# A fused attention and gated-MLP block: paired crossbar transposes of the gate/up results, TensorE kept busy before the first tile, and a replanned engine order

## The chip, the cores and the metric

The kernel runs on one core of a Trainium2 chip. Five engines work side by side, each through its own instruction queue in the order in which the queue was filled: TensorE (PE) for matmuls, ScalarE (ACT) for activations, VectorE (DVE) for elementwise work, GpSimd (POOL) for small jobs, and SyncE (SP), which here only issues DMA transfers. An instruction waits on semaphores until what it needs is done, and everything behind it in its queue waits too. The metric is the time of one execution on the device in microseconds; lower is better.

## The reference

A block of one sequence of 2048 tokens with 1024 features, in bfloat16. First comes attention with 32 query heads of width 32 that share one key and one value head, then a gated MLP with 3584 hidden features. Both have a layer norm ahead and a residual around them:

```python
x = A_x                                   # [1, 2048, 1024]
n = layernorm(x)
q, k, v = n @ wq, n @ wk, n @ wv          # q: 32 heads of 32; k and v: one head of 32
p = softmax(q k^T * 32**-0.5)
h = x + concat(p v) @ wo
m = layernorm(h)
out = h + (sigmoid(m @ w_gate) * (m @ w_up)) @ w_down
```

## The kernel before, in words

The 2048 tokens are 16 tiles of 128. The program is first written as a plan: each operation is put in a list of its engine with what it depends on. A planner, the class `Plan`, gives each one a start and an end by durations that are written in the source, and so decides the order in every queue. Only the order and the dependencies reach the chip; planned idle time does not. `TUNE` holds the planner's settings, `LATE` and `SLOW` its corrections for the landing of DMA transfers. `late` is added to every planned landing.

**Head.** Each x tile is loaded, its mean and variance are taken (`stats`), it is centered (`center`, L386) and scaled (L393 or L398). The first four tiles are transposed on PE against an identity (`mk_xT`, L457), the rest by a DMA through the crossbar (L401). From the transposed tiles PE makes K and V (`mk_KV`) and the queries (`mk_Qc`, `mk_Q`).

**Middle.** Attention goes over 512 visits: 32 half tiles of queries (128 tokens by 16 of the 32 heads, 2048 columns in all) by 16 key tiles. A visit (`emit_S`) is four matmuls of 32 rows by 512 columns that run side by side in the four row groups of the array, here called an S round. They fill four PSUM banks with scores, and two ACT instructions of 1024 columns take the exponential of them (L690) into a slot of `Pr`. There are six such banks, so an S round waits for the first exp of the visit before it. DVE adds the exps up (`make_add`, L665). PE multiplies them with V in four column groups (`mk_PV`), sums the partial sums with a small selection matrix (`mk_SUM`), and the reciprocal goes through DRAM (`r_scratch`) to be spread over the partitions (`rb`). `OT` is the product (L748), and `mk_OP` the output projection. Then come the second layer norm and a transposing DMA into `hnT` (`load_hT`).

Between the S rounds PE works on the MLP of earlier tiles. One pass is the MLP of one token tile. It has seven groups of 512 hidden features, each with a gate half and an up half (`mk_GU`), so 14 halves. A half needs one slab of weights of 1 MB, loaded in four pieces (L929) into a ring of four slabs. Odd passes go through the groups in reverse order, and the slabs of a pass's last two groups are kept for the next. A gate half ends with a tanh on ACT (L972), an up half with a product on DVE (L988) into a staging buffer `act_s`. From there a transposing DMA (L991) takes it to `hact`. The first pass and the last two work with the transposed product instead and need no such DMA (`held_w`). The down projection (`mk_D`) takes four pieces of 28 matmuls of 256 columns from `hact` and `wd_sb`; DVE adds each to the residual (L1025), and the rows are stored.

All these groups take one of two PSUM banks (`F_ps`) and are picked by the loop at the end of the kernel. It asks at each step whether an S round can go, or which group's inputs are known to be there by the plan. When a pass starts, `start_ffn` puts due marks for the previous tile's down pieces: a piece comes up when no more gate/up halves are left than its mark plus `d_off`.

**Tail.** After the last S round what remains is the last half tile's sums and output projection and the MLP of the last tiles.

The product that ends an up half, and the DMA behind it:

```python
so = act_s[:, k % NST, :]
e = pl.op("dve", lambda: DVE.scalar_tensor_tensor(
    out=so, in0=tnh[:, :], scalar=1.0, in1=F_ps[:, b, :],
    op0=ALU.add, op1=ALU.mult), [last, box["a"], act_dma.get(k - NST)], prio=0, **t_dve(512))
done = act_dma[k] = dma(lambda: SP.dma_start_transpose(ho, so), ...)
```

Of the kernel before, what the change touches and what calls it, by code (L numbers as in the profile page):

```python
# [12 lines left out]
P = 128  # L13
# [2 lines left out]
SEM = 75.0  # L16


TUNE = dict(late=100, ws0=1, ws1=2, parts0=3, parts1=4, lord=2, h_ord=0, ho=0, ho2=3, pvl1=0, pvl2=0, col_ok=0,
            pace0=310, swait=100, parts=2, raw=1, rl=0, nd=4, pc=16, rate=315, pace=310, xd=4, qf=1, dall=1,  # L20
            wo_late=1, nkn=1, few=1, rmin=600, hmin=1, h0=0, h1=350, hf=1.0, run=700, sum_few=1, pv_few=4,
            d_off=2, d_a=1, d_b=1, eb=0, eq=100)


class Op:
# [16 lines left out]
class Plan:  # L42
# [3 lines left out]
    LATE = {"sl": 465.0, "hT": -90.0, "xt": 100.0, "wd": -100.0, "xr": -300.0, "rb": -250.0, "ql": -500.0, "qs": -200.0,  # L46
            "o": -500.0, "wo": 700.0, "x": -435.0}

    SLOW = {"rb": 1.9, "ha": 2.5, "ql": 1.6, "wq": 1.1}

    def __init__(self):
        self.lists = {e: [] for e in ("pe",) + self.ENG}
        self.free = {e: 0.0 for e in ("pe",) + self.ENG}
        self.heap = {e: [] for e in self.ENG}
        self.dma_free = 0.0
        self.pace_free = 0.0
        self.pe_mode = "dense"
        self.hold = (0.0, 0.0)
        self.t_last = 1e12
        self.seq = 0  # L60

    def op(self, eng, fn, deps=(), order=(), occ=60.0, lat=None, prio=5, key=None, nbytes=0, pace=False, tag=None):
        self.seq += 1
# [38 lines left out]
    def step(self, limit):  # L102
        best = None
        for e in self.ENG:
            h = self.heap[e]
            if h:
                s = min(self.start_of(o) for o in h)
                if best is None or s < best[0]:
                    best = (s, e)
        if best is None or (limit is not None and best[0] > limit):  # L110
            return False
        s, e = best
        h = self.heap[e]
        o = min((o for o in h if self.start_of(o) <= s + 1e-9), key=lambda o: (o.prio, o.seq))
        h.remove(o)
        if o.pace and self.pace_free > s:
            s2 = self.pace_free
            prev = [a for a in self.lists["act"][-6:] if a.end <= s2]
            if prev:
                o.deps.append(prev[-1])  # L120
            s = s2
        self.free[e] = s + o.occ
        o.start = s
        if o.nbytes:
            if o.pace:
                self.pace_free = s + o.nbytes / TUNE["pace0" if self.fast(s) else "pace"]
            k = o.key.rstrip("0123456789_")
            go = max(s + 1720.0, self.dma_free)
            self.dma_free = go + o.nbytes * self.SLOW.get(k, 1.0) / TUNE["rate"]
            o.end = self.dma_free + 700.0 + self.LATE.get(k, 0.0) + TUNE["late"]  # L130
        else:
            o.end = s + o.lat
        o.pos = len(self.lists[e])
        self.lists[e].append(o)
        for u in o.users:
            u.ready = max(u.ready, o.end)
            u.missing -= 1
            if u.missing == 0:
                self.heap[u.eng].append(u)
        o.users = []  # L140
        return True
# [21 lines left out]
def bass_sequential_preLN__grouped_kv_mqa__glu_gated_glu__prompt_kernel(  # L163
# [20 lines left out]
    NH = NT * 2  # L184
    NB = 3
    NHB = 3
    NST = 3
    NSLAB = 4
    SW = 512
    NGR = NFT // 4  # L190
# [4 lines left out]
    with ExitStack() as es:  # L195
# [3 lines left out]
        def SB(name, shape, dt=BF16):  # L199
            return EC(nc.sbuf_tensor(name, [P] + shape, dt))  # L200

        ident = SB("ident", [P])
# [11 lines left out]
        rb = SB("rb", [512], F32)  # L214
# [4 lines left out]
        hnT = SB("hnT", [DT, 2, P])  # L219
        hact = SB("hact", [NFT * 256])  # L220
        tnh = SB("tnh", [512], F32)
        act_s = SB("act_s", [NST, 512])
        st = SB("st", [8, 2, 6], F32)
        mv = SB("mv", [2, NT, 2], F32)
        mvb = SB("mvb", [2, NT, 2])
# [8 lines left out]
        F_ps = EC(nc.psum_tensor("F_ps", [P, 2, 512], F32))  # L234
# [28 lines left out]
        PE, ACT, DVE, POOL, SP = nc.tensor, nc.scalar, nc.vector, nc.gpsimd, nc.sync  # L263

        def dma(fn, key, nbytes, deps=(), prio=5, pace=False, order=(), occ=450.0):
            return pl.op("sp", fn, deps, occ=occ, key=key, nbytes=nbytes, prio=prio, pace=pace, order=order)
# [9 lines left out]
        def both(out_ap, in_ap):  # L276
# [7 lines left out]
        c_id = pl.op("pool", lambda: POOL.affine_select(  # L284
            out=ident[:, :], in_=ident[:, :], compare_op=ALU.not_equal, fill=1.0, base=0,
            pattern=[[-1, P]], channel_multiplier=1), [c2], occ=300)
# [89 lines left out]
        sv1 = {}  # L376
        xnorm = {}
        xcent = {}

        def center(t):  # L380
            if t >= TUNE["pc"]:
                xcent[t] = pl.op("pool", lambda t=t: POOL.tensor_scalar(
                    out=x_sb(t), in0=x_sb(t), scalar1=mvr[:, 0, t, 0:1], scalar2=None, op0=ALU.subtract),
                    [sv1[t][0]], prio=2, occ=1150, lat=1300)
            else:
                xcent[t] = pl.op("dve", lambda t=t: DVE.tensor_scalar(  # L386
                    out=x_sb(t), in0=x_sb(t), scalar1=mvr[:, 0, t, 0:1], scalar2=None, op0=ALU.subtract),
                    [sv1[t][0]], prio=2, occ=330, lat=500)

        def make_norm1(t, deps):  # L390
            dst, src, sc = xn[:, t % 2, :], x_sb(t), rstd[:, 0, t:t + 1]
# [4 lines left out]
        def x_by_dma(t):  # L396

            xnorm[t] = pl.op("dve", lambda: DVE.tensor_scalar(  # L398
                out=x_sb(t), in0=x_sb(t), scalar1=rstd[:, 0, t:t + 1], scalar2=None, op0=ALU.mult),
                [xcent[t], sv1[t][1]], prio=1, occ=330, lat=500)  # L400
            xT_ev[t] = dma(lambda: SP.dma_start_transpose(xnT[:, t // 4, :, (t % 4) * P:(t % 4 + 1) * P], x_sb(t)),  # L401
                           f"xt{t}", P * D * 2, [xnorm[t]], prio=0, occ=1250.0)
            ring_free(t)
            queue_after_xT(t)
            if t == NT - 1:
                load_wo()
# [6 lines left out]
        for tiles in ([0], [1], [2, 3], [4, 5], [6, 7], [8, 9], [10, 11], [12, 13], [14, 15]):  # L413
            after = ((), ())
            if tiles[0] in (1, 2):

                p = tiles[0] - 1
# [19 lines left out]
        def mm(o, l, r, start, stop, **kw):  # L437
            return lambda: PE.matmul(o, lhsT=l, rhs=r, start=start, stop=stop, **kw)  # L438

        def pe_op(fn, n, mode, deps, last_of_round=True):  # L440
            if mode != pl.pe_mode:
                pl.free["pe"] += SWITCH
                pl.pe_mode = mode
            if mode == "dense":
                occ = max(25.0, n / 2.4 + 2.4)
            else:
                occ = max(25.0, n / 2.4 + 2.4) - 10.5 if last_of_round else 3.5
            return pl.op("pe", fn, deps, occ=occ, lat=max(25.0, n / 2.4 + 2.0) + 170.0 + SEM)


        xT_ev = {}
# [448 lines left out]
        def group_of(p, i):  # L900
            return i if p % 2 == 0 else NGR - 1 - i
# [35 lines left out]
        hact_ev = {}  # L937
        box = {}

        act_dma = {}  # L940
        n_act = [0]

        def gu_deps(t):
            return [d_last[t - 2]] if t >= 2 else q_store[-NQS:] if t else extra_rel
# [4 lines left out]
        def mk_GU(t, i):  # L949


            gr = group_of(t, i)
            held_w = t < TUNE["ws0"] or t >= NT - TUNE["ws1"]
            ho = hact[:, :].rearrange("p (a f b) -> p a f b", a=2, b=P)[:, t % 2, 4 * gr:4 * gr + 4, :]
# [22 lines left out]
            def after_u(b, last):  # L977
                if held_w:
                    e = pl.op("dve", lambda: DVE.scalar_tensor_tensor(
                        out=ho, in0=tnh[:, :].rearrange("p (f b) -> p f b", b=P), scalar=1.0,  # L980
                        in1=F_ps[:, b, :].rearrange("p (f b) -> p f b", b=P),
                        op0=ALU.add, op1=ALU.mult), [last, box["a"]] + gu_deps(t), prio=0, **t_dve(512))
                    done = e
                else:
                    k = n_act[0]
                    n_act[0] += 1
                    so = act_s[:, k % NST, :]
                    e = pl.op("dve", lambda: DVE.scalar_tensor_tensor(  # L988
                        out=so, in0=tnh[:, :], scalar=1.0, in1=F_ps[:, b, :],
                        op0=ALU.add, op1=ALU.mult), [last, box["a"], act_dma.get(k - NST)], prio=0, **t_dve(512))  # L990
                    done = act_dma[k] = dma(lambda: SP.dma_start_transpose(ho, so), f"ha{t % 2}_{gr}", P * 1024, [e] + gu_deps(t),  # L991
                                            prio=0, occ=700.0)
                box["e"] = e
                for f in range(4):
                    hact_ev[(t, 4 * gr + f)] = done
                free(1, last)
                if i == NGR - 1:
                    gu_last[t] = last
                    load_hT(t + 2)
                    for dq in range(ND):  # L1000
                        queues["D"].append(mk_D(t, t, dq))
                return [e]
# [63 lines left out]
        while True:  # L1066
            t = pl.free["pe"]
# [204 lines left out]
```

## Time and profile before

| | us |
|---|---|
| time, median of 3 (1107.64 to 1110.86) | 1107.84 |
| span of the profiled execution | 1107.7 |
| PE busy | 1079.6 |
| ACT busy | 1007.6 |
| DVE busy | 842.7 |
| exp on ACT (L690), 1008 of the 1024 | 947.2 |
| gate/up matmuls of 512 columns, 1456 | 362.2 |
| down-projection matmuls, 1792 | 228.6 |
| S matmuls, 2048 | 202.0 |

Instructions of one engine overlap in the pipeline, so the sum of single durations is above the time that a group takes. The 16 DMA engines are busy for 78.2% of the span with the queue that SyncE fills, and 232.92 MB move. The TensorE clock that the throttle granted is full in all slices.

### The profile page before, as it was taken

How to read it: one execution, taken by the hardware profiler on the slowest of the kernel's cores; microseconds unless marked ns; L12 is line 12 of the kernel's file. 1: busy time of each engine (PE TensorE's matmuls, PEld its weight loads, DVE VectorE, ACT ScalarE, POOL GpSimd, SP SyncE). 2: the span in 40 equal slices, each digit the busy share in tenths (PEclk: the TensorE clock that was granted, in tenths of full speed). 3: DMA queues.
4: the chain of work that ended last, by engine and by line, in shares of the span. 5: the costliest groups of instructions: out<-in, count | busy, mean ns of one | idle time of the engine just before them, and what ended most of it. 6: DMA issues, size and time to landing. Idle time of an engine off the chain costs nothing.

```text
span 1107.7 us, 25728 instructions
## 1 busy us (share of the span) xinstructions
PE 1079.6 (97%) x10616; PEld 531.7 (48%) x10616; DVE 842.7 (76%) x1051; ACT 1007.6 (91%) x1155; POOL 65.5 (6%) x93
## 2 busy tenths in 40 slices
PE   6899999999999999999999999999999999999999
PEld 5533365444444444444444443444444444445898
DVE  7979888787878778787878778787877778787311
ACT  4999999999999999999999999999999999998010
POOL 3300000010100001010100101010100101010000
PEclk9999999999999999999999999999999999999999
DMA  8693499787978697696879697697879778686992
GB/s 243 119 314 121 119 322 263 221 218 187 237 186 220 171 263 194 194 226 185 233 178 245 162 241 201 180 221 207 222 186 245 187 201 219 176 227 186 295 324 74
DMA packets 294053, 232.92 MB, mean 210 GB/s; under 512 B 97072, under 2 KB 280368, under 8 KB 293936
## 3 DMA queue, kind: packets, MB, share of 16 engines
q1 hardware_dynamic: 293936, 231.28, 78.2%
q8 instruction: 84, 1.38, 0.5%
q14 instruction: 33, 0.27, 0.1%
HBM read 203.82 MB, written 8.12 MB: 191 GB/s over the span
## 4 chain that ended last, share of the span: by engine, by line
PE 54%; ACT 34%; DMA 5%; DVE 4%; issue 2%; SPq 1%; POOL 0%; DVEq 0%
PE F_ps L438 45%; ACT Pr L690 32%; PE S_ps L438 8%; DMA ring<-in_B_w_up_dram 3%; ACT tnh L972 2%; DVE acc L665 1%; DVE st L342 1%; DMA r_scratch<-r_sb 1%; DVE st L344 0%; DMA zone<-ring 0%; DVE ring L398 0%; DVE ring L386 0%; DMA ring<-in_A_x_dram 0%; DMA rb<-r_scratch 0%; DVE r_sb L731 0%
## 5 line engine op out<-in xcount | busy, mean ns | idle before, releaser
L690 ACT ACTIVATE Pr<-S_ps 128x1024 bf16<-128x1024 f32 x1008 | 947.2, 1076 | 8.0 <-PE S_ps L438 7.5
L665 DVE TENSOR_TENSOR acc<-acc,Pr 128x2048 bf16<-128x2048 bf16 x429 | 524.0, 1221 | 78.4 <-ACT Pr L690 63.3
L438 PE MATMUL F_ps<-ring,hnT 128*128 128x512 bf16 x1456 | 362.2, 381 | 3.9 <-DMA ring<-in_B_w_up_dram 3.0
L438 PE MATMUL F_ps<-zone,hact 128*128 128x256 bf16 x1792 | 228.6, 273 | 0.0
L438 PE MATMUL S_ps<-QTb,kT 32*128 32x512 bf16 x2048 | 202.0, 384 | 5.2 <-ACT Pr L690 3.3
L438 PEld LDWEIGHTS F_ps<-ring,hnT 128*128 128x128 bf16 x1456 | 123.3, 97 | 171.6 <-issue 53.1
L438 PEld LDWEIGHTS F_ps<-zone,hact 128*128 128x128 bf16 x1792 | 163.1, 98 | 63.4 <-issue 32.7
L438 PEld LDWEIGHTS S_ps<-QTb,kT 32*128 32x128 bf16 x2048 | 51.5, 91 | 179.8 <-ACT Pr L690 132.9
L438 PE MATMUL F_ps<-Pr,Vt 128*32 128x512 bf16 x2016 | 135.2, 382 | 0.5 <-DVE Vt L278 0.5
L972 ACT ACTIVATE tnh<-F_ps 128x512 f32<-128x512 f32 x112 | 72.4, 646 | 61.9 <-PE F_ps L438 61.9
L438 PE MATMUL F_ps<-zone 128*128 128x512 bf16 (+3 forms) x584 | 78.5, 281 | 3.9 <-DVE mvb L351 1.4
L988 DVE SCALAR_TENSOR_TENSOR act_s<-tnh,F_ps 128x512 bf16<-128x512 f32 x91 | 62.3, 685 | 22.5 <-PE F_ps L438 20.9
L438 PEld LDWEIGHTS F_ps<-Pr,Vt 128*32 128x32 bf16 x2016 | 43.8, 95 | 60.8 <-issue 28.5
L438 PE MATMUL F_ps<-wo_sb,OT 128*128 128x512 bf16 x256 | 63.6, 381 | 2.0 <-DVE OT L748 1.5
L365 POOL TENSOR_SCALAR zb<-mvb 128x1 bf16<-128x1 bf16 (+1 forms) x23 | 6.0, 260 | 970.0 <-DVE mvb L351 970.0
L438 PE MATMUL F_ps<-hnT,ring 128*128 128x128 bf16 x912 | 61.0, 219 | 0.9 <-DMA ring<-in_B_w_gate_dram 0.7
L438 PEld LDWEIGHTS F_ps<-hnT,ring 128*128 128x128 bf16 x912 | 52.4, 98 | 9.3 <-issue 7.6
L438 PEld LDWEIGHTS F_ps<-zone 128*128 128x128 bf16 x584 | 40.5, 100 | 34.1 <-issue 11.2
L790 DVE TENSOR_TENSOR oun<-F_ps,oun 128x512 f32<-128x512 f32 x34 | 23.5, 691 | 39.8 <-PE F_ps L438 39.8
L1025 DVE SCALAR_TENSOR_TENSOR h_sb<-F_ps,h_sb 128x256 bf16<-128x256 f32 x64 | 26.8, 419 | 30.2 <-PE F_ps L438 30.2
L731 DVE RECIPROCAL r_sb<-F_ps 128x64 f32<-128x64 f32 x31 | 17.3, 558 | 30.8 <-PE F_ps L438 30.7
L438 PEld LDWEIGHTS F_ps<-wo_sb,OT 128*128 128x128 bf16 x256 | 20.9, 97 | 34.4 <-issue 13.1
(73 smaller groups left out, 408.3 us busy)
## 6 DMA issues: line engine op xcount, KB each, us to landing
ring<-in_B_w_gate_dram SPq DMA_DIRECT2D x308, 256.0 KB, 4.7
ring<-in_B_w_up_dram SPq DMA_DIRECT2D x304, 256.0 KB, 4.3
rb<-r_scratch SPq DMA_DIRECT2D x124, 64.0 KB, 2.3
zone<-in_B_w_down_dram SPq DMA_DIRECT2D x14, 512.0 KB, 5.5
Pr<-in_B_w_up_dram SPq DMA_DIRECT2D x24, 256.0 KB, 5.3
Pr<-in_B_w_gate_dram SPq DMA_DIRECT2D x20, 256.0 KB, 5.5
ring<-in_A_x_dram SPq DMA_DIRECT2D x16, 256.0 KB, 5.7
h_sb<-in_A_x_dram SPq DMA_DIRECT2D x16, 256.0 KB, 4.2
```

Source lines behind the costliest of these rows:

```text
L342: a = pl.op("dve", lambda s=s, src=src: DVE.bn_stats(st[:, s, 0, :], src[:, 0:512]), dp, prio=prio, occ=600, lat=756, order=[st_user.get(s ...
L365: f = pl.op("pool", lambda: POOL.tensor_scalar(out=zb[:, ph, tk], in0=mvb[:, ph, tk, 1], scalar1=LN_EPS_BF16, scalar2=None, op0=ALU.add), ...
L438: return lambda: PE.matmul(o, lhsT=l, rhs=r, start=start, stop=stop, **kw)
L665: add_op[(hf, kt)] = pl.op("dve", lambda: DVE.tensor_tensor(out=a, in0=in0, in1=slot, op=ALU.add), dp, prio=6, **t_dve(2048, 1.92))
L690: exps[u] = pl.op("act", lambda i=i, pb=pb: ACT.activation(out=slot[:, i * 1024:(i + 1) * 1024].rearrange("p (a b) -> p a b", a=2), in_=S_ ...
L731: rc = pl.op("dve", lambda: DVE.reciprocal(r_sb[:, :], F_ps[:, b, 0:64]), [last, rd_ld.get(hf - 1)], prio=0, occ=64 * 8 / 0.96 + 20, lat=6 ...
L790: oun_ev[(hf, part)] = pl.op("dve", lambda: DVE.tensor_tensor(out=o, in0=F_ps[:, b, :], in1=o, op=ALU.add), [last, oun_ev[(hf, part - 1)]] ...
L972: box["a"] = pl.op("act", lambda: ACT.activation(out=tnh[:, :], in_=F_ps[:, b, :], func=ACTF.Tanh, scale=0.5), [last, box.get("e")], prio= ...
L988: e = pl.op("dve", lambda: DVE.scalar_tensor_tensor(out=so, in0=tnh[:, :], scalar=1.0, in1=F_ps[:, b, :], op0=ALU.add, op1=ALU.mult), [las ...
L1025: e = pl.op("dve", lambda: DVE.scalar_tensor_tensor(out=h_sb[:, t % NHB, sl], in0=F_ps[:, b, 0:DW], scalar=0.5, in1=h_sb[:, t % NHB, sl], ...
```

## The change

Three things are done together.

1. The results of two neighbouring gate/up groups go into one staging buffer of 1024 columns, and one transposing DMA takes both to `hact`. The seventh group goes alone. There are two such buffers (`NST = 2`) in place of three of half the width. It is meant to halve the number of transposes.
2. Right after the identity matrix is made, PE runs 70 matmuls of 128 columns on it into an unused bank. They are to keep it busy until the first x tile comes.
3. The planner's settings and durations are new. The planned landings are later by 300 ns (`late`), a planned gate/up half waits for two weight pieces (`nkn=2`), planned pacing of weight loads is slower (`pace`), the order of DVE's work on the first two tiles is another (`ho`, `ho2`), and the marks for the down pieces are another (`d_off`, `d_a`, `d_b`). With them the order in all queues is planned anew.

```diff
-TUNE = dict(late=100, ws0=1, ws1=2, parts0=3, parts1=4, lord=2, h_ord=0, ho=0, ho2=3, pvl1=0, pvl2=0, col_ok=0,
-            pace0=310, swait=100, parts=2, raw=1, rl=0, nd=4, pc=16, rate=315, pace=310, xd=4, qf=1, dall=1,
-            wo_late=1, nkn=1, few=1, rmin=600, hmin=1, h0=0, h1=350, hf=1.0, run=700, sum_few=1, pv_few=4,
-            d_off=2, d_a=1, d_b=1, eb=0, eq=100)
+TUNE = dict(warm=70, late=400, ws0=1, ws1=2, parts0=3, parts1=4, lord=2, h_ord=0, ho=3, ho2=0, pvl1=0, pvl2=1,
+            col_ok=1, pace0=310, swait=400, parts=2, raw=1, rl=0, nd=4, pc=16, rate=315, pace=280, xd=4, qf=1,
+            dall=0, wo_late=1, nkn=2, few=1, rmin=900, hmin=1, h0=0, h1=600, hf=1.35, run=700, sum_few=2,
+            pv_few=4, d_off=1, d_a=-1, d_b=-1, eb=150, eq=1000)
...
-    SLOW = {"rb": 1.9, "ha": 2.5, "ql": 1.6, "wq": 1.1}
+    SLOW = {"rb": 1.9, "ql": 1.6, "wq": 1.1}
...
+        self.free["sp"] = self.free["pool"] = 700.0
...
-            self.dma_free = go + o.nbytes * self.SLOW.get(k, 1.0) / TUNE["rate"]
+            w = self.SLOW.get(k, 1.0) if k != "ha" else 2.5 if o.nbytes < 200000 else 1.3
+            self.dma_free = go + o.nbytes * w / TUNE["rate"]
...
-    NST = 3
+    NST = 2
...
-        act_s = SB("act_s", [NST, 512])
+        act_s = SB("act_s", [NST, 1024])
...
-                    [sv1[t][0]], prio=2, occ=330, lat=500)
+                    [sv1[t][0]], prio=2, occ=392, lat=560)
...
-                [xcent[t], sv1[t][1]], prio=1, occ=330, lat=500)
+                [xcent[t], sv1[t][1]], prio=1, occ=392, lat=560)
...
+        for i in range(TUNE["warm"]):
+            pe_op(mm(F_ps[:, 1, 0:P], ident[:, :], ident[:, :], True, True), P, "dense", [c_id] if i == 0 else [])
...
+                    j = i // 2
+                    members = [group_of(t, x) for x in (2 * j, 2 * j + 1) if x < NGR]
+                    g0, n = min(members), len(members)
                     k = n_act[0]
-                    n_act[0] += 1
-                    so = act_s[:, k % NST, :]
+                    if gr == members[-1]:
+                        n_act[0] += 1
+                    so = act_s[:, k % NST, (gr - g0) * 512:(gr - g0 + 1) * 512]
...
-                    done = act_dma[k] = dma(lambda: SP.dma_start_transpose(ho, so), f"ha{t % 2}_{gr}", P * 1024, [e] + gu_deps(t),
-                                            prio=0, occ=700.0)
+                    if gr == members[0] and n == 2:
+                        box["p"] = e
+                        done = None
+                    else:
+                        src = act_s[:, k % NST, 0:512 * n]
+                        hv = hact[:, :].rearrange("p (a f b) -> p a f b", a=2, b=P)[:, t % 2, 4 * g0:4 * (g0 + n), :]
+                        done = act_dma[k] = dma(lambda: SP.dma_start_transpose(hv, src), f"ha{t % 2}_{g0}_{n}", P * 1024 * n,
+                                                [e] + ([box["p"]] if n == 2 else []) + gu_deps(t), prio=0, occ=1245.0)
```

More of the change, by code (lines that the diff above doesn't have):

```diff
@@ L990, in after_u @@
                         op0=ALU.add, op1=ALU.mult), [last, box["a"], act_dma.get(k - NST)], prio=0, **t_dve(512))
-                    done = act_dma[k] = dma(lambda: SP.dma_start_transpose(ho, so), f"ha{t % 2}_{gr}", P * 1024, [e] + gu_deps(t),
-                                            prio=0, occ=700.0)
+                    if gr == members[0] and n == 2:
[6 more added lines that the diff above has]
+                                                [e] + ([box["p"]] if n == 2 else []) + gu_deps(t), prio=0, occ=1245.0)
+                        for g in members:
+                            for f in range(4):
+                                hact_ev[(t, 4 * g + f)] = done
+                if held_w:
+                    for f in range(4):
+                        hact_ev[(t, 4 * gr + f)] = done
                 box["e"] = e
-                for f in range(4):
-                    hact_ev[(t, 4 * gr + f)] = done
                 free(1, last)
```

## The prediction

> **What bounds the kernel now.** I read the page's busy shares and slices first, then the waits, then the head and the tail in the timeline, and last the spacing of single instructions.
>
> ```profile
> PE 1079.6 (97%) x10616; PEld 531.7 (48%) x10616; DVE 842.7 (76%) x1051; ACT 1007.6 (91%) x1155; POOL 65.5 (6%) x93
> ...
> PE   6899999999999999999999999999999999999999
> ...
> ACT  4999999999999999999999999999999999998010
> ```
>
> ACT is full from the second slice to the 37th and then nearly empty. So there are three parts. The head ends at the first S matmul (15.08 us), the middle at the last one (1019.95), and the tail is everything after. They last 15.1, 1004.9 and 87.7 us. The change has to be priced in each.
>
> ```profile
> PEld S_ps L438 <- ACT Pr L690: 132.9, 355, 1.4
> ...
> PEld F_ps L438 <- DMA ring<-in_B_w_up_dram: 12.4, 19, 1.3
> ```
>
> These are waits. Most S rounds wait for an exp to free their PSUM banks, so PE usually leads ACT. But in the trace's starts the lead is short. An S round that waited stands 1.28 us after the start of the exp that freed its banks. The next visit's first exp comes 0.54 us after that S at the most, and never under 0.446 us. So PE leads by only 0.1 us: a visit with 0.12 us too much matmul shows at once as idle ACT. The second line is a different wait: gate/up matmuls that stand for weights still in flight.
>
> ```profile
> 684.92 1.90 PE L438 MATMUL F_ps<-ring,hnT 128*128 128x512 bf16 x8
> 687.30 0.39 PE L438 MATMUL F_ps<-ring,hnT 128*128 128x512 bf16 x1 [0.48 <-DMA ring<-in_B_w_up_dram]
> 687.62 0.39 PE L438 MATMUL S_ps<-QTb,kT 32*128 32x512 bf16 x4
> 687.95 0.39 PE L438 MATMUL F_ps<-ring,hnT 128*128 128x512 bf16 x1
> 688.62 0.60 PE L438 MATMUL F_ps<-ring,hnT 128*128 128x512 bf16 x2 [0.28 <-DMA ring<-in_B_w_up_dram]
> ```
>
> In the timeline of PE the S round stands behind the late gate/up matmul in the fixed order, so a late slab delays the exps too.
>
> **A ledger of the middle.** The middle has 512 visits of one S round. From starts in the trace: a dense matmul takes 216 ns (512 columns), 109 (256) or 56 (128); a round of four packed PV or S matmuls 216; a change between packed and dense 100; about 15 more per visit. ACT takes 911 per exp and 480 per tanh. I count each visit's matmuls from the instruction order, start S no sooner than 1.28 us after the previous visit's first exp, and the exp no sooner than 0.446 us after S. For the kernel before this gives PE 983, ACT 983 and 994.5 us for both together; 64 visits in the steady part give 124.8, and the trace has 125.1 to 127.2. It puts idle ACT where the trace has it (visits 266, 268, 273: 107, 121, 73 ns by ledger, 115, 114, 66 measured). The 10.4 us that it leaves out are 3.4 in the first 64 visits and 7.0 later. The later part is almost the 6.9 us by which 20 gate/up matmuls start later than their spacing, nearly all waiting for weights.
>
> [...] 128-column matmuls start 107 ns apart until 14.2 us and 56 apart after 15.4. [...] weight pieces of 256 KB land 2.8 to 6.0 us (5th to 95th percentile) after issue.
>
> **Head: +0.3.** 70 constant matmuls start when the identity is ready (1.8 us). Priced at 107 ns until the clock rises, and 56 after, [...] I take 8.8, with about the 6.3 us that the clock took in this trace. The first x tile's transposes started at 8.02:
>
> ```profile
> 8.02 1.03 PE L457 MATMUL F_ps<-ident,zone 128*128 128x128 bf16 x8 [8.02 <-DVE zone L393]
> ...
> 9.88 4.64 PE L438 MATMUL F_ps<-zone 128*128 128x128 bf16 x48 [0.83 <-issue]
> ```
>
> Warm, this stretch gives back some 2.5 us (about 48 spacings of 51 ns saved). But the new order (ho=3) puts a BN_STATS of tile 1 (0.61) before tile 0's aggregation, and tile 1's centering before the copy out of PSUM. It also puts tile 1's transposes and K/V (16 further matmuls of 128 columns, then 8 of 32) and two DVE copies ahead of the first S. Following the DVE list by its measured durations, the second Q copy ends near 15.2. First S at 15.1 to 15.8, I take 15.4; the bounds for the sum are -0.5 and +1.2.
>
> **Middle: -5.7.** Three edits act here.
> - The new order: 1136 mode changes where there were 1160, and 29 fewer down-projection matmuls before the last S. PE's ledger falls to 977. Four small evacuations leave ACT (18 to 14, two of them 512 wide), so ACT's falls to 982. Both together: 993.8 against 994.5. The steady 64 visits stay at 124.8: the cuts fall differently, but their imbalances are as large. So the order itself gives 0.7.
> - Pairing: 91 transposes become 39 of two groups and 13 of one. SyncE spent 1.2 us issuing each, so 39 x 1.2 = 47 us of its queue go. The transpose also waits in that queue for its DVE result (62.9 us over 55 waits), with weight loads queued behind it. A pair needs the width of the hnT transpose, which lands in 5.4 us, against 4.1 for one group. The first half also waits for the second group, some 9 us (two of 14 slabs in a 62.8 us pass). The down projection waits for that, but its first piece now starts with 11 of 14 gate/up halves left, where it was 13: three slabs of 4.5 us after the pass, so I price it at nothing. The two wider staging buffers wait for a transpose issued one pair earlier, again some 9 us: nothing.
> - Later planned landings (100 to 400 ns, a first wait for two weight pieces, down-projection pieces spread evenly between slabs): PE gets other work where it stood. Taking 0.3 us off each of the 20 late starts leaves 1.9 of the 6.9 us. Slower planned pacing (310 to 280) is in the same plan. Bounds: all gone, or all kept.
>
> Keeping the 3.4 of the first visits and 0.1 unexplained: 993.8 + 3.4 + 1.9 + 0.1 = 999.2, against 1004.9.
>
> **Tail: +2.4.** PE is dense here, with one gap of size, for the softmax sums' trip through DRAM.
>
> ```profile
> 1034.47 1.11 PE L438 MATMUL F_ps<-hnT,Pr 128*128 128x128 bf16 x17
> 1037.06 1.89 PE L438 MATMUL F_ps<-wo_sb,OT 128*128 128x512 bf16 x8 [1.48 <-DVE OT L748]
> ```
>
> After the last S stand 318 down-projection matmuls where there were 289; the rest is equal: 29 x 109 ns = +3.2. Between the sums and the output projection now lie 29 of 256 columns and 128 of 128, with the sums' own matmuls 10.8 us, against a need of 11.7, so the 1.64 us gap falls to about 0.9. The last hidden state landed 9.5 us after the projection; 128 x 56 + 28 x 109 ns = 10.2 us cover it. +3.2 - 0.8 = +2.4, bounds 1.5 and 3.5.
>
> Sum: 1107.84 + 0.3 - 5.7 + 2.4 = **1104.8 us**.
>
> **Rivals.**
> - Weights as late as before. For it: the loads wait for PE to free a slab (168 us in SyncE's waits), and no more slabs are given; the wait could move with the plan. Against it: the stalls are 0.2 to 0.95 us, the size of the new margin. Then only the ledger's 0.7 counts: 1107.84 + 0.3 - 0.7 + 2.4 = 1109.8.
> - The start smooths out as well. For it: ACT loses 3.4 us to copies and cold matmuls in the first 64 visits, and the plan has new durations there (392 for 330). Against it: DVE is 43 of the first 50 us busy and gets four more copies. With 2 of the 3.4 gone and the late weights all gone: 1104.8 - 3.9 = 1100.9.
> - Slower: paired transposes land late and down-projection matmuls stand at the head of PE's queue, with S behind them. 0.6 us in each of 14 passes is 8.4 us, on top of the first rival's stalls: 1118. Against it: the three slabs of distance.
>
> **How the numbers follow.** Chances: forecast 0.46, weights as late 0.24, smooth start 0.19, slower 0.11. The head's, tail's and stalls' bounds spread each case by some 3 us. The range goes from below the smooth start to above the first rival, 1099 to 1111; it leaves out most of the slow case. The bound of 0.3% is 3.3 us, so 1104.5 and 1111.2. Half of the forecast's case and most of the smooth start fall below: 0.43. Slower: the slow case and the edge of the first rival, 0.13. The rest, 0.44, is no change.
>
> **What would show it.** In the changed kernel's profile: PEld waiting on DMA for ring under 5 us (it was 12.4) and PE's late gate/up starts near 2; first S at 15.4; middle at 999; tail at 90; 128-column matmuls at 56 ns from the first x tile on. Wrong it is if 64 visits in the steady part take over 125.5 us, if PE waits on the hact transposes, or if the tail has a new gap at the output projection.

## The result and the profile after

The changed kernel takes 1100.66 us (median of 4, 1100.54 to 1102.65). The kernel before, measured beside it, takes 1108.08 us (1107.64 to 1110.86). The ratio is 0.9932, 95% interval 0.9912 to 0.9952, so the kernel is faster by some 7.4 us. The forecast was 1104.8.

The profiled executions can be cut at the first and the last S matmul, and once more at S round 64 (rounds are counted from 0). The first two columns are moments, in us from the start of the span, so the second contains the first; the next two are lengths.

| | first S at | S round 64 at | from there to the last S | tail | span |
|---|---|---|---|---|---|
| before | 15.08 | 141.41 | 878.5 | 87.7 | 1107.7 |
| after | 13.54 | 137.13 | 871.8 | 89.8 | 1098.7 |
| difference | -1.5 | -4.3 | -6.7 | +2.1 | -8.9 |

The spans differ by more than the medians, as the profiled execution of before was one of 1109.46 us, 1.6 above its median. Of the 4.3 us at S round 64, 3.2 are there at S round 12 already.

The page of the kernel after, busy shares and slices:

```profile
PE 1077.9 (98%) x10686; PEld 542.1 (49%) x10686; DVE 834.5 (76%) x1055; ACT 1003.8 (91%) x1151; POOL 65.4 (6%) x93
...
PE   7899999999999999999999999999999999999999
...
ACT  4999999999999999999999999999999999998110
```

The shape is the old one: full from the second slice on, with ACT leaving in the 37th. PE's 70 more matmuls are the constant ones. The page's shares do not show where 9 us went. The waits of the kernel after do (engine, what it waited for: us in total, times, longest):

```profile
PEld S_ps L440 <- ACT Pr L696: 146.4, 380, 1.7
...
PEld F_ps L440 <- DMA ring<-in_B_w_gate_dram: 0.2, 1, 0.2
```

The weight loads' wait for the slabs, 12.4 us in 19 for the up halves before, is gone; 0.2 us is all that is left of this kind. PE's wait for a freed score bank is longer (132.9 before), as it should be: PE comes to the S round sooner and stands for ACT, not the other way round. Measured by the starts in the trace, gate/up matmuls that begin later than their usual spacing ("late gate/up starts") fall from 6.9 us in 20 to 0.1 in 2. That is nearly the whole 6.7 us of the third column.

The head of the kernel after, PE's timeline (start, duration, what, idle before it and its releaser):

```profile
1.84 5.58 PE L440 MATMUL F_ps<-ident 128*128 128x128 bf16 x70 [1.84 <-POOL ident L286]
7.83 0.62 PE L463 MATMUL F_ps<-ident,zone 128*128 128x128 bf16 x8 [0.42 <-DVE zone L395]
...
13.54 0.40 PE L440 MATMUL S_ps<-QTb,kT 32*128 32x512 bf16 x4
...
16.90 1.95 PE L440 MATMUL F_ps<-zone 128*128 128x128 bf16 x32 [1.35 <-DMA zone<-in_A_wq_dram]
```

The constant matmuls end 0.4 us before the first x tile is there, eight transposes take 0.62 us where they took 1.03, and the first S comes 1.5 us sooner. But three us later PE stands 1.35 us for the query weights, until 16.90.

The tail of the kernel after:

```profile
1028.80 2.46 PE L440 MATMUL F_ps<-zone,hact 128*128 128x256 bf16 x21
1031.33 1.90 PE L440 MATMUL F_ps<-wo_sb,OT 128*128 128x512 bf16 x8
```

The output projection follows the down projection with no idle time to speak of; before it waited 1.48 us for `OT`.

### The profile page after: what moved, and what is told of

It is laid out like the page before. It is cut to its first block, busy times and chain, and to the rows that moved or that the text cites. A ratio compares the mean times of both kernels' runs of the same rounds, so it can differ in the third digit from the quotient of the medians.

```text
span 1098.7 us, 25839 instructions
## 1 busy us (share of the span) xinstructions
PE 1077.9 (98%) x10686; PEld 542.1 (49%) x10686; DVE 834.5 (76%) x1055; ACT 1003.8 (91%) x1151; POOL 65.4 (6%) x93
## 3 DMA queue, kind: packets, MB, share of 16 engines
q8 instruction: 84, 1.38, 0.5%
## 4 chain that ended last, share of the span: by engine, by line
ACT 43%; PE 37%; issue 7%; DVE 6%; DMA 6%; SPq 2%; POOL 0%; DVEq 0%
ACT Pr L696 40%; PE F_ps L440 31%; PE S_ps L440 5%; DMA rb<-r_scratch 3%; DVE acc L671 3%; ACT tnh L978 2%; DMA r_scratch<-r_sb 2%; SPq L740 1%; DMA ring<-in_A_x_dram 1%; DVE st L346 1%; DMA hnT<-hn 1%; DVE st L344 0%; DVE h_sb L860 0%; DVE ring L400 0%; DVE OT L754 0%
## 5 line engine op out<-in xcount | busy, mean ns | idle before, releaser
L440 PE MATMUL F_ps<-zone,hact 128*128 128x256 bf16 x1792 | 224.5, 273 | 0.0
L440 PE MATMUL F_ps<-Pr,Vt 128*32 128x512 bf16 x2016 | 138.0, 382 | 0.6 <-DVE h_sb L860 0.2
L440 PE MATMUL F_ps<-zone 128*128 128x512 bf16 (+3 forms) x584 | 75.7, 274 | 4.9 <-DMA zone<-in_A_wq_dram 1.4
L440 PEld LDWEIGHTS F_ps<-Pr,Vt 128*32 128x32 bf16 x2016 | 46.3, 95 | 63.0 <-issue 28.4
L985 DVE SCALAR_TENSOR_TENSOR hact<-tnh,F_ps 128x512 bf16<-128x512 f32 x21 | 14.4, 686 | 33.0 <-PE F_ps L440 33.0
```

What stands on the lines that cost most here:

```text
L985: e = pl.op("dve", lambda: DVE.scalar_tensor_tensor(out=ho, in0=tnh[:, :].rearrange("p (f b) -> p f b", b=P), scalar=1.0, in1=F_ps[:, b, : ...
```

## The experiments

Two readings stood against each other. The first is that of the prediction: pairs take transposes and their waits out of SyncE's queue, and the later planned landings give a margin, and both together end the weight waits; the start is worth little. The rival: the start is worth as much, and the weight waits end for one of these reasons alone. Each run below changes one thing in the source; where it is a setting of the planner, the order of many operations changes with it. "Round 64" is the start of S round 64 in the trace. Each run is compared with the kernel before on the same chip, and each trace is of one execution.

**The constant matmuls, taken out and put in.** The new kernel without them, orders otherwise equal:

```diff
-            pe_op(mm(F_ps[:, 1, 0:P], ident[:, :], ident[:, :], True, True), P, "dense", [c_id] if i == 0 else [])
+            pe_op(lambda: None, P, "dense", [c_id] if i == 0 else [])
...
+                if ins is None:
+                    continue
```

> The changed kernel without its 70 constant matmuls; every queue keeps its order. If the early clock is what moved the first S round (15.08 to 13.54 us), 128-column matmuls run 107 ns apart again until about 14 us and the first S comes at 15.5 to 16, the whole 1.5 to 2.5 us later: about 1102.5 us. If the new order of VectorE's work moved it, the first S stays within 0.5 us of 13.5 and the whole within 0.7 us of 1100.7. Middle and tail unchanged in both.

Measured: 1101.28 us, ratio to before 0.9915 (0.9888 to 0.9943). PE's timeline:

```profile
8.15 1.01 PE L463 MATMUL F_ps<-ident,zone 128*128 128x128 bf16 x8 [8.15 <-DVE mvb L353]
9.99 2.93 PE L440 MATMUL F_ps<-zone 128*128 128x128 bf16 x32 [0.83 <-POOL dsb L362]
...
15.17 0.40 PE L440 MATMUL S_ps<-QTb,kT 32*128 32x512 bf16 x4
```

The eight transposes take 1.01 us again, where it was 0.62 with the constants, and the first S is back at 15.17, 1.64 us later. Yet round 64 starts at 136.9, where it starts at 137.1 with the constants. PE's timelines show where the gain goes; two lines without the constants, then one with them:

```profile
17.12 1.96 PE L440 MATMUL F_ps<-zone 128*128 128x128 bf16 x32
19.77 0.40 PE L440 MATMUL S_ps<-QTb,kT 32*128 32x512 bf16 x4 [0.69 <-DVE QTb L280]
```

```profile
19.36 0.40 PE L440 MATMUL S_ps<-QTb,kT 32*128 32x512 bf16 x4 [0.51 <-DVE QTb L280]
```

Without constants PE comes to the query matmuls at 17.12 and finds their weights there; with them it stands until 16.90. So the third S round is only 0.41 us sooner, and soon nothing is left. The same kernel a second time, beside a second run of the kernel after:

> The changed kernel without the constant matmuls once more, beside the changed kernel on one chip. If the early clock is worth nothing at the end, the two times agree within 0.1% (1 us), with a first S some 1.5 us later and the first 64 visits as much shorter. If it is worth its 1.6 us, the ratio to the kernel before is 0.9946 or more where the changed kernel has 0.9932.

> The changed kernel itself, for comparison on the same chip. Every theory: 0.9932 of the kernel before, first S near 13.5 us, middle 995 to 996, tail near 90.

Measured: 1101.07, ratio 0.9930 (0.9917 to 0.9942), without; 1100.52, ratio 0.9934 (0.9921 to 0.9948), with. The other way round, the kernel before with the 70 matmuls at the front of PE's list:

```diff
+        lists["pe"][0:0] = [Op("pe", mm(F_ps[:, 1, 0:P], ident[:, :], ident[:, :], True, True),
+            [c_id] if i == 0 else [], [], 0.0, 0.0, 0, 0, None, 0, False, None) for i in range(70)]
```

> The kernel before with 70 constant matmuls put ahead of PE's list; nothing else moves. Clock theory: 128-column matmuls 56 ns apart from the first tile on, the second Q group then bound by its weights (landed at 11.4 us), first S at 12.9 instead of 15.1 and the whole about 2 us shorter, 1106. Rival (VectorE and the loads set the start): first S within 0.5 us of 15, the whole unchanged.

Measured: 1108.93 against 1110.03, ratio 0.9990 (0.9978 to 1.0001), with the first S at 13.42. In all three comparisons the constants move the first S by 1.3 to 1.7 us and the total by less than the intervals. They do not say quite the same: in the old order the lead is not given back early. There round 64 starts at 139.98, against 141.41 before and 140.63 in the kernel with pairing alone, whose PE order is that of before. A gain of up to 2 us in the total is inside the interval, so for the old order it stays open.

**Pairing alone.** The kernel before with the pairs of the new one, and nothing else in the source: old settings, old durations. The orders of PE and ACT come out identical to those of before. Those of DVE and SyncE do not: `OT` stands one place earlier on DVE in 13 of its 32 places, and in about as many passes the write of the reciprocals and a few weight loads change places on SyncE.

> The kernel before with paired transposes alone: old planner settings, PE's order as before, 52 transposes. If fewer transposes are the cause, the late gate/up starts fall from 6.9 us to under 2 and the whole by 4 to 6, to 1103. If the plan's margin is the cause, they stay at 5 or more and the whole within 1.5 us of 1108.

Measured: 1103.68 us, ratio 0.9943 (0.9920 to 0.9967), 6.4 below the 1110.03 of its own comparison. First S 14.27, round 64 at 140.6, then 873.1, tail 87.9. (The head is not changed, so 0.8 us of difference in the first S is what two executions can show.) Waits of this kernel, PEld's for the weights and SyncE's for the transposes:

```profile
PEld F_ps L439 <- DMA ring<-in_B_w_up_dram: 4.3, 7, 1.3
...
SPq L1007 <- DVE acc L670: 62.6, 36, 3.2
```

Late gate/up starts fall from 6.9 to 2.0 us. SyncE stands as long for DVE as before (62.9 us in 55), but at 36 places where it was 55. So pairing gives most of the gain without any margin in the plan, and it gives most of that after round 64 (5.4 us).

**The new plan alone.** All new settings and the constant matmuls, but each group with its own transpose, and planned so:

> All of the new settings, the constant matmuls too, but every group transposed by a DMA of its own, and planned so (91 transposes, three buffers). Ledger of the middle 992.7 us (993.8), tail 0.8 longer. If the new settings alone keep the weights ahead, late gate/up starts under 1 us, a span of 1098 to 1100. If the 39 transposes fewer are needed, late starts of 4 us or more and a span of 1102 to 1105.

Measured: 1101.17 us, ratio 0.9932 (0.9917 to 0.9947): what the whole change gives. It has 91 transposes, SyncE waits 75.4 us in 52 for their data, and the weight loads do not mind (PEld's waits):

```profile
PEld F_ps L440 <- DMA ring<-in_B_w_gate_dram: 0.3, 1, 0.3
```

Late gate/up starts are 0.3 us, and from round 64 to the last S it takes 871.7, the kernel after 871.8. So the two remedies overlap: pairing alone takes 6.4 us off, the plan alone 7.7 and both together 8.4 (1101.17 and 1100.52 against one 1108.89). The ratios of the last two cannot be told apart. Pairing alone is a little behind: on its chip it took 1102.54 to 1107.05, and the new kernel without constants 1100.13 to 1101.90. It lacks what the plan gives before round 64.

**The number of transposes, in both orders.** In the new kernel each pair is issued as two single transposes, one behind the other, at the place of the pair:

```diff
-done = act_dma[k] = dma(lambda: SP.dma_start_transpose(hv, src), ...)
+done = act_dma[k] = dma(lambda: [SP.dma_start_transpose(hv[:, 4 * m:4 * m + 4, :],
+                                 src[:, 512 * m:512 * m + 512]) for m in range(n)], ...)
```

> The changed kernel with every pair's transpose issued as two of one group, one after the other, at the pair's place in the queue; all other orders as they are (91 transposes again). If fewer transposes are why no gate/up matmul waits for weights any more, PE's late gate/up starts come back (0.1 us to 4 or more) and the whole takes 3 to 6 us more. If the plan's later landings and the new places of the down pieces are why, late starts stay under 1 us and the whole within 1 us of 1100.7.

Measured: 1103.56, ratio 0.9951 (0.9936 to 0.9966). Late gate/up starts stay at 0.3 us. From round 64 to the last S it takes 874.2 us, 2.4 more than the kernel after; 1.3 of it is in one block of 64 rounds (192 to 255), where an output projection begins 0.8 us late, and the rest is spread in parts of 0.1 to 0.4 that were not traced. The interval overlaps that of the kernel after on another chip. But on the same chip the new kernel without constants took at most 1101.90 and this one at least 1102.87, so some 2 us are likely real: the single transposes cost a little here too, and not by weight waits. The same edit in the kernel with pairing alone:

> The kernel before with pairing, in which each pair is issued as two single transposes, one behind the other, at the place of the pair; the engines' orders are those of the kernel with pairing alone (1103.7 us, late gate/up starts 2.0 us, weight loads 4.3 us behind the queue), and the number of transposes is 91 again. Theory A (it is the number of transposes, at 1.2 us of SyncE each, that held the weight loads back): late gate/up starts come back to 5 us or more, weight waits to 7 us or more, ratio to the kernel before 0.998 to 1.001, about 1107. Theory B (it is that SyncE has only about every second gate/up group a transpose to wait for, so that weight loads behind it are issued earlier): late starts stay at or under 2.5 us and the ratio is 0.993 to 0.997, about 1104 to 1105.

Measured: 1114.29, ratio 1.0049 (1.0033 to 1.0064), slower than before, and outside what either theory expected. The engines' orders are those of pairing alone. Its waits (up halves' weights, and the path of the softmax sums):

```profile
DVE OT L753 <- DMA rb<-r_scratch: 53.4, 28, 3.4
...
PEld F_ps L439 <- DVE oun L791: 13.6, 13, 1.2
...
PEld F_ps L439 <- DMA ring<-in_B_w_up_dram: 1.2, 4, 0.4
```

The weights are in time (late starts 0.4 us), so theory A fails. But `OT` waits 53.4 us for the reciprocals from DRAM; it was 14.3 before and 23.9 with pairs. Two stretches of the timeline of this run show how, SyncE's first and PE's second:

```profile
714.40 4.40 SPq L1007 DMA_TRANSPOSE hact<-act_s  x2
718.89 0.54 SPq L738 DMA_DIRECT2D r_scratch<-r_sb  x1
```

```profile
729.84 1.04 PE L439 MATMUL F_ps<-wo_sb,OT 128*128 128x512 bf16 x4 [0.80 <-DVE act_s L998]
...
732.91 0.82 PE L439 MATMUL F_ps<-wo_sb,OT 128*128 128x512 bf16 x3 [0.74 <-DVE oun L791]
```

SyncE issues two transposes in 4.4 us (the longest of the 39 times; the median is 2.5) where one pair took 1.26, and the write of the reciprocals stands behind them. From the reciprocal on DVE to `OT` the median grows from 9.3 us with pairs to 10.6. It was 10.1 in the kernel before, where one output projection began late, so 10.6 is just more than the fixed order leaves. So the output projection comes late, and S behind it: 11.0 us of PE's time at 17 output projections in the middle. SyncE's time per transpose (1.19 to 3.14 us each in this run, median 1.26) was paid on the way of the sums, not by the weight loads. Theory B is not shown by this run either: PE's new stalls give the slabs more time to land, so the small weight waits may be their effect.

**The margin alone, and the new kernel without it.** One setting, `late`, 100 to 400 in the kernel before, and 400 to 100 in the new one:

> The kernel before, planned with landings 300 ns later and nothing else; 91 transposes. Counted from the order the middle's ledger falls to 988.7 us (994.5) and the tail grows by 17 us (30 matmuls of 512 columns, 47 of 256 and 96 of 128 more after the last S round). If the plan's margin is enough to end the waits for weights, late gate/up starts fall from 6.9 us to under 2 and the span is 1114. If only fewer transposes end them, they stay at 5 or more and the span is 1119.

Measured: 1124.05, ratio 1.0146 (1.0126 to 1.0165); the trace is of the fastest execution, 1121.56. PEld still waits 10.6 us for weight slabs in 21, where it was 13.2 in 20:

```profile
PEld F_ps L438 <- DMA ring<-in_B_w_up_dram: 7.2, 16, 0.8
PEld F_ps L438 <- DMA ring<-in_B_w_gate_dram: 3.4, 5, 1.4
```

From round 64 to the last S the trace takes 873.4, 5 less than before, but the plan has moved work behind the last S (the ledger of the middle is 5.8 shorter): the tail grows from 87.7 to 106.5. (Some 1% of this trace's matmul records are missing, so its late starts are not counted.)

> The changed kernel, planned with landings 300 ns sooner, transposes paired. Ledger of the middle 994.9 (993.8), tail 3.7 longer. If pairing is enough by itself, late gate/up starts stay under 2 us and the span is 1104. If the margin is needed, they come back to 5 us and the span is 1108 to 1109.

Measured: 1110.60, ratio 1.0022 (1.0010 to 1.0034), a span near 1108.8 and so what was expected if the margin is needed. The trace is of a slower execution, 1112.49. Rounds 192 to 511 keep their pace (124.7 to 124.9 us per 64, the last 64 122.8): there the pairs and the rest of the plan do without the margin. It loses most at one place in the first MLP pass and in the tail (93.8, 4.0 more). The first pass works without transposes to `hact`, so there pairs cannot help. PE's timeline at that place:

```profile
184.05 0.28 PE L440 MATMUL F_ps<-hnT,ring 128*128 128x128 bf16 x2
186.91 1.14 PE L440 MATMUL F_ps<-hnT,ring 128*128 128x128 bf16 x9 [2.58 <-DMA ring<-in_B_w_up_dram]
187.99 0.61 PE L440 MATMUL S_ps<-QTb,kT 32*128 32x512 bf16 x4
```

An S round takes 0.61 us where it took 0.40, for 6.8 us after the wait. Three stretches of this run's time (bounds, length; busy us and count of PE, PEld, DVE, ACT, POOL; granted clock, DMA share, GB/s):

```profile
182.00:186.40 4.40, 1.80 (x21) 0.78 (x18) 0.23 (x1) 4.40 (x6) 0.00 (x0) 1.00 1.17 268
186.40:193.20 6.80, 6.29 (x79) 3.85 (x83) 3.69 (x5) 3.43 (x5) 0.00 (x0) 0.50 0.86 251
193.20:196.00 2.80, 2.80 (x48) 1.50 (x40) 1.97 (x3) 2.25 (x4) 0.00 (x0) 1.00 0.71 173
```

The granted clock is 0.50 after the wait: one late slab cost more here than its 2.6 us. All twelve executions of this kernel show a mean clock a little under full (0.995 to 0.998). The 64 rounds that hold it take 130.8 us, 5.1 more than those of the kernel after (125.7).

**The first wait for two weight pieces** (`nkn` 2 to 1 in the new kernel):

> The changed kernel with a gate/up half planned to start when one of its four weight pieces has landed by the plan, where it was two. Ledger of the middle 990.2 (993.8), tail 2.1 longer: 1.6 us less, a span of 1097.2, if the other margins keep the weights ahead. If the second piece was needed, late gate/up starts of 2 to 5 us and a span of 1099 to 1102.

Measured: 1102.12, ratio 0.9952 (0.9938 to 0.9967). PEld waits 1.7 us in 4 for weight slabs, against 0.2 in 1. The middle takes 995.0, though the ledger of this order has 990.2; what the rest of these 4.8 us is was not traced. The tail is 92.5. Nothing is won or lost beyond the intervals.

**The query copies** (`eq` 1000 to 100 in the new kernel, so the planner may give copies of queries out of PSUM to ACT again; in the first 110 us ACT makes 14 copies of queries in this trace, 10 in that of the kernel after and 13 in that of before):

> The changed kernel with the old preference for ScalarE in copying queries out of PSUM (eq back to 100). Theory: taking these copies off ScalarE is what shortened the first 64 visits; the ledger puts them 1.9 us longer (123.1 for 121.2), the tail 0.8 longer, the later visits 1.1 shorter, the span 1100.3. Rival: the first visits are set by loads and VectorE, and the first 64 visits stay within 0.5 us of 123.6.

Measured: 1105.84, ratio 0.9976 (0.9959 to 0.9992). First S 13.65, but round 64 at 141.8, against 137.1. The first 64 rounds take 128.1 us, so neither expectation holds. A part of the 4.6 us is a stretch at half clock again (0.53 in the mean from 45.4 to 49.0). PE's timeline of this run:

```profile
42.74 0.40 PE L440 MATMUL F_ps<-Pr,Vt 128*32 128x512 bf16 x4
45.31 0.27 PE L440 MATMUL F_ps<-zone 128*128 128x256 bf16 x1 [2.18 <-DMA zone<-ring]
45.51 0.61 PE L440 MATMUL S_ps<-QTb,kT 32*128 32x512 bf16 x4
```

What PE waits for is a transposed x tile, which comes late in this order; the run does not tell the copies' own cost from that. A second wait, of 1.93 us at 171.2, is followed by another 3.4 us at half clock (0.50 from 171.8 to 175.2). The traced execution took 1108.73 us, 2.9 above the median. The four of twelve with a full clock throughout took 1103.15 to 1105.02, so some 3 us of the loss are there without any half clock.

## Why the prediction was right or wrong

The range held the time, but the point was 4.1 us too high, and the result lies on the second rival (1100.9). That rival's number is in part luck: it has the late weights all gone, as they were, but 2 us off the excess of the first visits where 1.0 came off, and the head and the choice of the traced execution (below) make up for it.

- **Head, +0.3: wrong by 1.9 us in its number, and in the new order without effect on the time.** The failing step is the end of the second query copy, put at 15.2 by following the DVE list. It came at 13.44, and the first S at 13.54 for 15.4. Some 1.0 us of this is the clock (an estimate): the constants were taken to end at 8.8, but ended at 7.42, and the first transposes began at 7.83. The rest lies in the DVE list and was not traced. In the trace of the kernel after, the constants start 107 ns apart up to 5.01 us, 3.2 us after the first of them began, and 56 apart from there. I took 6.3, from the old trace. That the constants bring nothing in the end of the new order is shown by taking them out (1101.28, 1101.07); in the old order (ratio 0.9990) up to 2 us stay open.
- **First 64 rounds, an excess over the ledger kept at 3.4: mis-sized.** They took 123.6 us where they took 126.3. The order's own share of this is 1.7 by the ledger, which has 121.2; the excess over it fell to 2.4. The forecast left this smoothing to a rival with 0.19. In the traces round 64 starts at 136.8 to 138.1 in all runs with the new order and its `eq` (the kernel after, without constants, single transposes of both kinds, `nkn`, `late`), and at 139.8 to 141.8 in those without. So the gain is the new order's, and it needs `eq`; how much is the copies' own is open.
- **Late weights, 6.9 to 1.9: right in kind, mis-sized, and for a reason that does not hold.** They fell to 0.1. The term was worked out as 0.3 us of margin for each of 20 starts. But pairing alone, with no margin, takes 4.9 us off, the margin alone leaves 10.6 of 13.2 us of weight waits (and makes the kernel slower by its tail), and the new plan without pairs takes all but 0.3 off. Pairs end most of these waits, and the plan nearly all. By which way pairing does it is not shown: SyncE's queue also has another order then. The price of pairing, "47 us of its queue", is right as a count (SyncE issues transposes for 119.1 us before and 68.8 after), but it says nothing of who is waiting: put back in the old order, this time was lost by the softmax sums.
- **Landing of pairs "at nothing": right.** PE waits on no transpose of `hact` in the kernel after; pairs land in 4.0 us and single ones in 2.9 (medians of 39 and 13), not the 5.4 that was taken from the `hnT` transpose. The third rival, 1118 with late pairs, has no support.
- **Ledger of the middle: right to 1 us.** The later 448 rounds take 871.8 us, the ledger has 872.6; a steady block takes 124.6, with 124.8 foreseen.
- **Tail, +2.4: right.** It grew by 2.1, with the gap at the output projection closed further than to 0.9.

In spans the head lies 1.9 us below the forecast, the middle 3.8 (1.8 late weights, 1.0 first rounds, 1.0 ledger and rest) and the tail 0.3, together 6.0. The time lies only 4.1 below, mostly as the parts were cut from an execution of before that was 1.6 slower than the median to which they were added.

One reading of the prediction is off, and nothing rests on it: weight pieces land 2.8 to 6.3 us after issue in the trace of before, not 2.8 to 6.0.

What stays open: which of the settings besides `late`, `nkn` and `eq` makes the new plan robust against late slabs. The order of the down pieces, the pacing, the DVE order of the first tiles and the settings that the text does not name were not tried singly.

## What to carry to other kernels

A wait that two remedies can end is worth its time once: try each alone before adding up their gains. Here the plan alone took 7.7 us off, the pairs alone 6.4 and both 8.4. When the pairs were split in the old order, SyncE's time was paid by `OT` (its wait for the reciprocals grew from 23.9 to 53.4 us) and not by the up halves' weights (4.3 to 1.2), so price a transfer's issue time by asking who is queued behind it at that place, not by its sum. An earlier first instruction may count only as far as the next limit: here 1.6 us at the first S round were 0.41 at the third, behind the wait for the query weights. Measure the gain behind that limit.

## What the runs showed of the hardware

In four places the clock granted to TensorE was half after a single idle stretch of PE: after 1.84 us (the kernel before with constants, at 312.7; 0.57 in the mean from 312.6 to 316.6), 1.93 and 2.18 us (the run with `eq` at 100; 0.50 from 171.8 to 175.2 and 0.53 in the mean from 45.4 to 49.0) and 2.58 us (`late` at 100; 0.50 from 186.4 to 193.2). Other single stretches were not followed by it: 1.38 us (the kernel after, at 63.1; 1.00 from 63 to 67), 1.48 us (the kernel before, at 1037.1; 1.00 from 1036 to 1041), 1.5 and 1.6 us ahead of an output projection (the second run without constants and the new plan alone; mean clock 1.0), and 2.07 us in the tail of the run with the margin alone (1.00 from 1030.3 to 1034.0). In that run waits of 0.75, 0.48 and 1.11 us ahead of three S rounds, at 182.5 to 186.7, were followed by 3.4 us at half clock (0.50 from 187.0 to 190.4), so the length of a single stretch is not all that counts. PE's lines of the shortest wait with half clock behind it and of the longest without, from the two runs:

```profile
312.66 1.00 PE L438 MATMUL F_ps<-ring,hnT 128*128 128x512 bf16 x3 [1.84 <-DMA ring<-in_B_w_up_dram]
```

```profile
1030.33 0.61 PE L438 MATMUL F_ps<-zone,hact 128*128 128x256 bf16 x4 [2.07 <-DMA hact<-act_s]
```

The lengths with and without it overlap, and how long the idle stretch may be was not tried by itself.

Issuing a crossbar transpose took SyncE 1.25 us for eight blocks of 128 by 128 and 1.21 for four (medians of 39 and 13 in the kernel after), so the price was nearly per transfer. With pairing alone and each pair split, 91 of four blocks took 1.19 to 3.14 us, with a median of 1.26.
